# One unit ahead of the second chunk's scores, and group 1's output products one step sooner

## The chip, the cores and the metric

The kernel runs on one core of a Trainium2 chip. A core has five engines with in-order instruction streams of their own: TensorE (matmuls and weight loads, PE and PEld in the profile), VectorE (DVE), ScalarE (ACT), GpSimd (POOL) and SyncE (SP); they are tied together by semaphores, and 16 DMA engines move data. Matmuls write into PSUM, which has eight banks of 512 float32 per partition. The metric is the device time of one execution in microseconds, the median of several.

## The reference

Two parts, one behind the other. A linear attention with a decay per head, in blocks of 64 tokens:

```
for each block b of 64 tokens:                       # q, k, v: [4, 8, 768, 64]
    intra = (qb kb^T * Dmask) vb                     # within the block, decayed by lam^(i-j)
    inter = (qb * lam^(i+1)) kv_state                # with all blocks before
    out[block] = intra + inter
    kv_state = lam^64 * kv_state + (kb * lam^(63-i))^T vb
x = out, heads side by side                          # [3072, 512]
h = x @ w_in                                         # [3072, 2048]
g = h + sin(alpha * h)^2 / (alpha + 1e-9)
result = g @ w_out                                   # [3072, 512], float32
```

## The kernel before

The 768 tokens of a sequence are cut into six chunks of 128 (t = 0 to 5), each of two blocks of 64. The chunk t of all four sequences makes group t of 512 tokens for the second part. So that TensorE always has something to do, the second part of group g runs beside the attention of chunk g + 1 (`t = g + 1`). All instructions are issued in an order that the program writes out by hand; each engine takes its own instructions in that order.

**The second part.** A group has 16 steps, one for each 128 of the 2048 hidden columns. `hidden(g, i)` (line 538) issues four matmuls of 512 columns into a PSUM bank `hps` (line 542), then a sine (547) and a square (552) on ScalarE; `finish(g, i)` (line 557) adds the hidden value and writes `gall` on VectorE (561), and thereby frees the bank. In group 1, banks 0 to 2 go round from step 4 on, so that step 12 takes the bank of step 9, step 13 that of step 10 and step 14 that of step 11; step 15 takes bank 4. The product with w_out is cut into *units*: `project(g, m, part)` (line 567) is four matmuls (572) for the m-th 128 tokens and the part-th quarter of the hidden columns; with part 3 the result is copied out and stored. Units wait in the list `behind`, and `run(n)` (line 687) issues the next n of them, wherever the program wants TensorE filled.

**The attention of a chunk**, in the order of its steps:

- loads of k, q, v through GpSimd's queue; k and q turned (heads to partitions) either by TensorE with a copy on ScalarE (`turns_pair`, lines 338 to 344) or by a DMA transpose from SyncE's queue (273);
- `pair_ready`: decayed keys on GpSimd (257); `states` (423): key-value products on TensorE; `update`: new state on VectorE (399, 403), decayed and cast on GpSimd (388, 392);
- `scores` (443): TensorE writes F_ps; `masks` (450): VectorE multiplies by the decay table and writes STm;
- output products into O_ps: those with the state (457) and those with the scores (482 or 505). For chunk 1 they are split over `outputs_first` and `outputs`; from chunk 2 on `outputs_in_one` (line 487 on) issues all, 64 of each kind. One product with the state is held until a small ScalarE copy of part of the turned q (`seen`, lines 472 and 516), a *fence*, which itself waits for the products issued ahead of it;
- `leave` (524): VectorE multiplies O_ps and writes x, the input of the next group (*x copies*), four for a chunk: pair 0 of the sequences and pair 1, each for two blocks.

**Chunk 1 (the second chunk).** Its attention runs between group 0 and group 1, in a straight list of calls (lines 722 to 751) with `run(n)` between them. After the last q is turned (`turns_pair(1, "q", 2, 5, (A, A))`) come its ScalarE copies, one unit, `update`, `scores`, `masks`, `outputs_first`, two units, `outputs`, `leave`, two units.

**Group 1 (with chunk 2).** For each step i the loop at line 802 issues what `feed` has for it, `hidden(1, i)`, what `slots` has for it, the units of this step, and `finish(1, i)`. Scores and masks come at steps 8 and 9 into and out of banks 4 to 7, which the output products use again. `hidden` takes a call `ahead`, which it makes between its four matmuls and its sine: at one step (`here`) of group 1 this is `outputs_in_one(2)`. Units come at steps 1, 3, 4, 8, 10 and 13; the one at step 13 multiplies the columns of steps 8 to 11. Groups 2 to 4 make the same call between sine and square of step 11 (`between`).

Of the kernel before, what the change touches and what calls it, by code (L numbers as in the profile page):

```python
# [15 lines left out]
def kernel(  # L16
# [16 lines left out]
    NT = S // T  # L33
# [61 lines left out]
    def load(t, nm, b0, b1):  # L95
        dst, src = NAT[nm]
        to = dst[t][:, b0:b1, :, :].rearrange("p b h e -> p (b h) e")
        by_head = src[b0:b1, :, t * T:(t + 1) * T, :].rearrange("b h p e -> p (b h) e")
        n = H * (b1 - b0)
        if t > 1 and nm != "v" and b0 == 2:  # L100
            nc.gpsimd.dma_start(out=to[:, 0:n - 1, :], in_=by_head[:, 1:n, :])
            nc.gpsimd.dma_start(out=to[:, n - 1:n, :], in_=by_head[:, 0:1, :])
        else:
            nc.gpsimd.dma_start(out=to, in_=by_head)  # L104
# [141 lines left out]
    def new_xt(t):  # L246
        xt[t] = xtp.tile([P, NDC, GRP], BF16, name="xt")
# [179 lines left out]
    def update(t, blk, pr):  # L427
        if blk and t == NT - 1:
            return
        new_state(blk, pr, att["KV", t, pr, blk], "fused" if t == blk == 1 else "decayed")  # L430
        if t > 1 and (t, blk) != (NT - 1, 0):
            decay_state(blk, pr)
        cast_state(blk, pr, home(t + 1, 0) if blk else home(t, 1))
# [40 lines left out]
    def outputs(t, prs=BOTH):  # L474
        inter(t, prs[0], 0, 0, 0, False)
        for pr in prs:
            for h0 in range(0, 2 * H, 2):
                for blk in range(2):
                    for n in (h0, h0 + 1):
                        half, m = where(t, pr, n)  # L480
                        u, h = n // H, n % H
                        nc.tensor.matmul(out=att["O", t, pr, blk][halves(h % 2), u, h // 2, :],  # L482
                                         lhsT=vn[t][halves(blk), 2 * pr + u, h, :],
                                         rhs=STm[t, pr][halves(blk), half, m // HP, m % HP, :],
                                         start=False, stop=True, skip_group_check=True)

    def outputs_in_one(t):
        banks_of("O", t, BOTH, None, "O_ps")
        regions = [(pr, h0 + j, blk) for h0 in range(0, 2 * H, 2) for blk in range(2) for pr in BOTH for j in range(2)]

        def meets(straight):
            return [(pr, blk, n) + where(t, pr, n) for pr, n, blk in regions
                    if (where(t, pr, n)[0] == blk) == straight]

        begun = set()

        def with_state(of):
            for pr, blk, n, half, m in of:
                inter(t, pr, half, m, blk, (pr, half, blk) not in begun)
                begun.add((pr, half, blk))  # L500

        def with_scores(of):
            for pr, blk, n, half, m in of:
                u, h = n // H, n % H
                nc.tensor.matmul(out=att["O", t, pr, blk][halves(h % 2), u, h // 2, :],  # L505
                                 lhsT=vn[t][halves(blk), 2 * pr + u, h, :],
                                 rhs=STm[t, pr][halves(blk), half, m // HP, m % HP, :],
                                 start=False, stop=True, skip_group_check=True)

        crossed, straight = meets(False), meets(True)  # L510
        sent = [r for r in crossed if (r[0], r[3], r[4]) == (0, 0, 0)]
        kept = [r for r in straight if (r[0], r[3], r[4]) == (0, 0, 0)]
        assert len(sent) == len(kept) == 1 and sent[0][1] == 1
        with_state([r for r in crossed if r not in sent] + sent)
        seen = QT[t][LO, 0, 0, 0:T:D]
        nc.scalar.copy(out=seen, in_=seen)
        with_state([r for r in straight if r not in kept])
        with_scores(straight)
        with_state(kept)
        with_scores(crossed)  # L520
# [158 lines left out]
    def queue_units(g, order):  # L679
        for m, part in order:  # L680
            def unit(g=g, m=m, part=part):
                project(g, m, part)
                if part == 3:
                    store(g, m)
            behind.append(unit)

    def run(n):
        for _ in range(min(n, len(behind))):
            behind.pop(0)()
# [46 lines left out]
    run(1)  # L736
    turns_pair(1, "q", 2, 5, (A, A))
    load(2, "k", 0, 2)
    run(1)
    update(1, 1, 1)  # L740
    scores(1, (1,), (5, 0))
    masks(1, 1)
# [1 line left out]
    outputs_first(1, (1,), (4, 2))  # L744
    load(2, "q", 0, 2)
    load(2, "q", 2, 4)
    run(2)
    outputs(1, (1,))
    leave(1, 1)
    run(2)  # L750
# [3 lines left out]
    def slots(g):  # L754
        t = g + 1
        d = {i: [] for i in range(NFC)}
        if g == 1:
            at = dict(KV=5, F=9, O=12)
        else:
            at = dict(KV=4, F=8, O=12)  # L760
        d[at["KV"]] += [(states, t)]
        for n in range(4):
            d[at["KV"] + ((0, 0, 1, 2)[n] if g == 1 else n)] += [(update, t, n // 2, n % 2)]
        if g == 1:
            d[8] += [(run, 1), (scores, 2), (masks, 2, 0)]
        else:
            d[at["F"]] += [(scores, t), (masks, t, 0)]
        d[at["F"] + (g > 1)] += [(masks, t, 1)]
        d[at["O"]] += [(leave, t, 0)]
        d[at["O"] + (g > 1)] += [(leave, t, 1)]  # L770
        return d

    def feed(g):
        t = g + 1
        d = {i: [] for i in range(NFC)}
        if g == 1:
            d[2] += [(turn_by_dma, 2, 0, "k"), (pair_ready, 2, 1), (decay_state, 1, 0), (decay_state, 1, 1), (turn_by_dma, 2, 1, "k"), (turn_by_dma, 2, 0, "q")]
            d[7] += [(put_held,), (turns_pair, 2, "q", 2, AB[0], (A, A))]
        if t + 1 < NT:
            if g == 1:  # L780
                d[6] += [(new_chunk, 3)] + [(load, 3, nm, b, b + 2) for nm, b in (("v", 0), ("k", 0), ("v", 2))]
                d[7] += [(load, 3, nm, b, b + 2) for nm, b in (("k", 2), ("q", 0), ("q", 2))]
            else:
                a = 6 if g == 2 else 2
                d[a] += [(new_chunk, t + 1)] + [(load, t + 1, nm, b, b + 2) for nm, b in (("v", 0), ("k", 0), ("v", 2))]
                d[a + 2] += [(load, t + 1, nm, b, b + 2) for nm, b in (("k", 2), ("q", 0), ("q", 2))]
            d[12] += [(turn_by_dma, t + 1, 0, "k"), (turn_by_dma, t + 1, 1, "k")]
            d[13] += [(pair_ready, t + 1, 0)]
            d[14] += [(turn_by_dma, t + 1, 0, "q"), (turn_by_dma, t + 1, 1, "q")]
            d[15] += [(pair_ready, t + 1, 1)]  # L790
        return d

    for g in range(1, NT + 1):
        if g < NT:
            gall[g] = gbp.tile([P, NFC, GRP], BF16, name="gall")
        at = slots(g) if g + 1 < NT else {}
        fd = feed(g) if g + 1 < NT else {}
        if g + 1 < NT:
            new_xt(g + 1)
        own = {8: (0, 0), 10: (0, 1), 13: (0, 2)} if g == 1 else {}  # L800
        units = [1, 3, 4, 10, 13] if g == 1 else [i for i in range(NFC) if g > 2 or i not in (0, 1, 3)]
        for i in range(NFC):
            if g == NT and not behind:
                break
            if i in own:
                queue_units(g, [own[i]])
            for a in fd.get(i, []):
                a[0](*a[1:])
            here = g + 1 < NT and i == (12 if g == 1 else 11)

            def unit_and_outputs():
                run(1)
                outputs_in_one(g + 1)

            if g < NT:
                hidden(g, i, unit_and_outputs if here and g > 1 else None,
                       (lambda: outputs_in_one(2)) if here and g == 1 else None)
            for a in at.get(i, []):
                a[0](*a[1:])
            if not (here and g > 1):  # L820
                run(units.count(i))
            if g < NT:
                finish(g, i)
        if g < NT:
            queue_units(g, [(m, part) for m in range(B - 1 if g == NT - 1 else B) for part in range(4)][len(own):])
# [31 lines left out]
```

## Time and profile before

| | |
|---|---|
| median of 3 runs (lowest to highest) | 207.53 us (207.43 to 207.54) |
| profiled execution | 207.3 us |
| its span, first to last instruction | 205.5 us |
| TensorE busy, matmuls | 197.5 us (96%) |
| ScalarE busy | 142.9 us (70%) |
| VectorE busy | 131.5 us (64%) |
| GpSimd busy | 106.7 us (52%) |
| granted TensorE clock, mean | 1.000 |

The profile is of one execution. Times in it are microseconds from the span's start. In a list in order of time, a row can hold several instructions of the same kind behind each other (x4), and the brackets tell how long the engine was idle before the row and whose end it waited for. A matmul's end is modelled and overlaps the next one's start: matmuls of 512 columns that follow each other start 0.216 us apart (20 from 70.17 to the next row at 74.49), though one is shown 0.38 us long. Some matmul records are missing, so a row of four can read x3.

### The profile page before, as it was taken

The numbers are of one execution on the slowest core, as the hardware profiler recorded it, in microseconds if no ns is written. First come the engines' busy times: TensorE is split into PE (matmuls) and PEld (weight loads), VectorE is DVE, ScalarE is ACT, GpSimd is POOL, SyncE is SP. The second block draws the span as 40 slices with busy tenths as digits, with TensorE's granted clock in tenths as the row PEclk, the third lists the DMA queues.
The fourth block names the chain that finished last, engine by engine and source line by source line (L and its number), as shares of the span: only waits on it lengthen the run. The fifth ranks groups of instructions, "written<-read, shape, count | busy, mean of one in ns | idle before, by whom it ended". The sixth has DMA issues, their size and how long they took to land.

```text
span 205.5 us, 5388 instructions
## 1 busy us (share of the span) xinstructions
PE 197.5 (96%) x2239; PEld 98.4 (48%) x2265; DVE 131.5 (64%) x219; ACT 142.9 (70%) x241; POOL 106.7 (52%) x112
## 2 busy tenths in 40 slices
PE   7899999999998999999999999999999999999994
PEld 2664455554453545455445454444454444444443
DVE  7695989473889769968557968555858544444000
ACT  7688997224999699676776676776676787887121
POOL 8989959988979973999976940002000000000000
PEclk9999999999999999999999999999999999999999
DMA  8999999999979999699999989601101101110213
GB/s 132 160 179 206 205 160 177 187 178 156 165 263 98 135 153 181 43 169 162 120 137 146 212 99 154 155 3 51 54 0 54 51 0 54 53 51 0 104 51 105
DMA packets 96683, 24.49 MB, mean 119 GB/s; under 512 B 87938, under 2 KB 94226, under 8 KB 96658
## 3 DMA queue, kind: packets, MB, share of 16 engines
q0 software_dynamic: 74528, 13.37, 86.8%
q1 hardware_dynamic: 22128, 10.76, 24.9%
q8 instruction: 18, 0.29, 0.6%
q14 instruction: 7, 0.06, 0.1%
q10 hardware_dynamic: 2, 0.00, 0.0%
HBM read 27.27 MB, written 6.29 MB: 163 GB/s over the span
## 4 chain that ended last, share of the span: by engine, by line
PE 88%; DMA 3%; ACT 2%; DVE 2%; POOL 2%; issue 1%; POOLq 0%; ACTq 0%
PE hps L542 38%; PE ops L572 38%; DMA qn<-in_q_dram 3%; PE O_ps L457 2%; PE hps L597 2%; PE KV_ps L423 2%; POOL kn L104 1%; PE F_ps L443 1%; DVE STm L450 1%; PE O_ps L505 1%; DVE gall L561 1%; PE hps L139 1%; ACT QKT L344 1%; ACT s_sb L547 1%; PE O_ps L363 1%
## 5 line engine op out<-in xcount | busy, mean ns | idle before, releaser
L561 DVE SCALAR_TENSOR_TENSOR gall<-s,r_sb,hps 128x512 bf16<-128x512 bf16 x96 | 71.1, 745 | 44.7 <-ACT s L552 44.5
L542 PE MATMUL hps<-xt,w_in 128*128 128x512 bf16 x370 | 94.0, 379 | 1.7 <-DVE gall L561 0.8
L572 PE MATMUL ops<-w_out,gall 128*128 128x512 bf16 x356 | 90.8, 379 | 1.1 <-issue 0.5
L547 ACT ACTIVATE s_sb<-hps,alpha_sb 128x512 bf16<-128x512 f32 x96 | 65.3, 684 | 29.6 <-PE hps L542 28.4
L552 ACT ACTIVATE s<-s_sb 128x512 bf16<-128x512 bf16 x91 | 57.3, 630 | 2.8
L542 PEld LDWEIGHTS <-w_in 128*128 128x128 bf16 x384 | 36.6, 98 | 44.0 <-issue 1.6
L572 PEld LDWEIGHTS <-gall 128*128 128x128 bf16 x368 | 34.9, 98 | 41.2 <-issue 0.6
L257 POOL TENSOR_TENSOR kdec<-kn,R 128x1024 bf16<-128x1024 bf16 x12 | 22.8, 1915 | 3.8 <-DMA kn<-in_k_dram 2.3
L392 POOL CAST sb<-S 128x512 bf16<-128x512 f32 x20 | 12.3, 619 | 21.1 <-DVE S L399 21.1
L388 POOL TENSOR_TENSOR SD<-S,L 128x512 f32<-128x512 f32 x16 | 16.7, 1049 | 8.6 <-DVE S L399 8.5
L524 DVE TENSOR_TENSOR xt<-O_ps,Etab 128x512 bf16<-128x512 f32 x20 | 12.8, 684 | 5.4 <-PE O_ps L482 4.4
L104 POOL DMA_DIRECT2D vn<-in_v_dram x13 | 14.6, 1122 | 0.0
L579 DVE COPY o_sb<-ops 128x512 f32<-128x512 f32 x15 | 10.3, 689 | 4.2 <-PE ops L572 4.1
L450 DVE TENSOR_TENSOR STm<-F_ps,C 128x512 bf16<-128x512 f32 x20 | 12.8, 683 | 0.3 <-PE F_ps L443 0.3
L581 ACT COPY o_sb<-ops 128x512 f32<-128x512 f32 x8 | 4.6, 577 | 12.0 <-PE ops L572 12.0
L399 DVE TENSOR_TENSOR S<-SD,KV_ps 128x512 f32<-128x512 f32 x16 | 10.8, 683 | 0.1
L104 POOL DMA_DIRECT2D kn<-in_k_dram x9 | 9.9, 1097 | 0.3 <-issue 0.3
L344 ACT COPY QKT<-T_ps 128x512 bf16<-128x512 bf16 x8 | 4.3, 584 | 5.3 <-PE T_ps L341 5.3
L139 PE MATMUL hps<-fill 128*128 128x256 bf16 (+1 forms) x24 | 6.5, 390 | 1.5 <-DVE fill L132 1.5
L104 POOL DMA_DIRECT2D qn<-in_q_dram x6 | 7.1, 1177 | 0.0
L356 DVE TENSOR_TENSOR STm<-F_ps,C 128x512 bf16<-128x512 f32 x8 | 5.2, 686 | 1.6 <-PE F_ps L352 1.5
L457 PEld LDWEIGHTS <-sb 64*64 64x64 bf16 x320 | 4.2, 107 | 3.0 <-issue 3.0
(95 smaller groups left out, 116.5 us busy)
## 6 DMA issues: line engine op xcount, KB each, us to landing
out_dram<-o_sb SPq DMA_DIRECT2D x19, 256.0 KB, 2.6
vn<-in_v_dram POOLq DMA_DIRECT2D x10, 256.0 KB, 8.1
w_out<-in_moe_w_out_dram POOLq DMA_DIRECT2D x4, 512.0 KB, 10.7
w_in<-in_moe_w_in_dram POOLq DMA_DIRECT2D x3, 512.0 KB, 9.8
kn<-in_k_dram POOLq DMA_DIRECT2D x6, 256.0 KB, 8.2
qn<-in_q_dram POOLq DMA_DIRECT2D x6, 256.0 KB, 9.0
out_dram<-o_sb SPq DMA_DIRECT2D x8, 128.0 KB, 1.8
kn<-in_k_dram POOLq DMA_DIRECT2D x4, 240.0 KB, 6.5
```

Source lines behind the costliest of these rows:

```text
L104: nc.gpsimd.dma_start(out=to, in_=by_head)
L257: nc.gpsimd.tensor_tensor(out=kdec[t][:, b0:b1, :, :], in0=kn[t][:, b0:b1, :, :], in1=R[:, o:o + H].unsqueeze(1).unsqueeze(3).broadcast_to ...
L388: nc.gpsimd.tensor_tensor(out=pair(SD, pr), in0=pair(S_of[n], pr), op=ALU.mult, in1=L64[:, pr].unsqueeze(1).unsqueeze(3).broadcast_to([P, ...
L392: nc.gpsimd.tensor_copy(out=pair(dst, pr), in_=pair(S_of[n], pr))
L399: nc.vector.tensor_tensor(out=S, in0=pair(SD, pr), in1=ps, op=ALU.add)
L450: nc.vector.tensor_tensor(out=st[:, hd], in0=att["F", t, pr, hd], op=ALU.mult, in1=of_mask(C64, t, pr, hd).unsqueeze(1).broadcast_to([P, 2 ...
L524: nc.vector.tensor_tensor(out=xview(t)[:, 2 * pr:2 * pr + 2, blk, :, :], in0=att["O", t, pr, blk], in1=Eb, op=ALU.mult)
L542: nc.tensor.matmul(out=hps[:], lhsT=w[:, c, (f % 4) * P:(f % 4 + 1) * P], rhs=xt[g][:, c, :], start=(c == 0), stop=(c == NDC - 1))
L547: nc.scalar.activation(out=s_sb[:], in_=hps[:], func=ACTF.Sin, scale=alpha_sb[:, f:f + 1])
L552: nc.scalar.activation(out=s2[:], in_=s_sb[:], func=ACTF.Square)
L561: nc.vector.scalar_tensor_tensor(out=gall[g][:, f, :], in0=s2[:], scalar=r_sb[:, f:f + 1], in1=hps[:], op0=ALU.mult, op1=ALU.add)
L572: nc.tensor.matmul(out=ops[:], lhsT=gall[g][:, f, m * P:(m + 1) * P], rhs=w_out_sb[part][:, f % 4, :], start=(f == 0), stop=(f == NFC - 1))
```

## The change

Two edits, both of order alone; every engine executes the same instructions as before.

In chunk 1, one of the two units between `outputs_first` and `outputs` moves to the place between the last turned q and the scores: two units there, one here.

In group 1, `outputs_in_one(2)` is called at step 11 instead of step 12, between the four matmuls of the step and its sine. On TensorE the output products thus stand ahead of step 12's matmuls; on ScalarE the fence's copy stands ahead of the twelfth sine (step 11) instead of the thirteenth. The x copies, all four ahead of the finish of step 12 before, become two ahead of the finish of step 11 and two ahead of that of step 12. The orders of GpSimd and SyncE do not change.

```diff
@@ chunk 1 @@
     turns_pair(1, "q", 2, 5, (A, A))
     load(2, "k", 0, 2)
-    run(1)
+    run(2)
     update(1, 1, 1)
     scores(1, (1,), (5, 0))
     masks(1, 1)
...
     load(2, "q", 2, 4)
-    run(2)
+    run(1)
     outputs(1, (1,))
     leave(1, 1)
@@ slots(g) @@
         if g == 1:
-            at = dict(KV=5, F=9, O=12)
+            at = dict(KV=5, F=9, O=11)
...
         d[at["O"]] += [(leave, t, 0)]
-        d[at["O"] + (g > 1)] += [(leave, t, 1)]
+        d[at["O"] + 1] += [(leave, t, 1)]
@@ loop over the steps @@
-            here = g + 1 < NT and i == (12 if g == 1 else 11)
+            here = g + 1 < NT and i == 11
```

## The prediction

> **What bounds the kernel now.** I read the page first: the shares of busy time and the slices of the span.
>
> ```profile
> span 205.5 us, 5388 instructions
> PE 197.5 (96%) x2239; PEld 98.4 (48%) x2265; DVE 131.5 (64%) x219; ACT 142.9 (70%) x241; POOL 106.7 (52%) x112
> PEclk9999999999999999999999999999999999999999
> PE 88%; DMA 3%; ACT 2%; DVE 2%; POOL 2%; issue 1%; POOLq 0%; ACTq 0%
> ```
>
> TensorE is busy for 96% of the span at full granted clock, and the chain of waits, the last line, runs through it for 88%. The change adds and removes no matmul, so it can only fill or open holes in TensorE's row. I therefore went to the order in time of each engine around the two edited places. Columns: start, duration, engine, line; in brackets the idle time before and its releaser. First the second chunk, between the last turned q and its output products:
>
> ```profile
> 42.41 1.04 PE L572 MATMUL ops<-w_out,gall 128*128 128x512 bf16 x4
> 43.64 0.45 PE L443 MATMUL F_ps<-QKT 64*64 64x64 bf16 x32 [0.20 <-ACT QKT L344]
> 44.74 1.67 PE L572 MATMUL ops<-w_out,gall 128*128 128x512 bf16 x7 [0.16 <-issue]
> 46.35 0.21 PE L457 MATMUL O_ps<-QKT,sb 64*64 64x64 bf16 x1
> ...
> 43.37 0.10 PEld L443 LDWEIGHTS <-QKT 64*64 64x64 bf16 x1 [0.42 <-issue]
> ...
> 42.52 1.07 ACT L344 COPY QKT<-T_ps 128x512 bf16<-128x512 bf16 x2 [3.00 <-PE T_ps L341]
> ...
> 44.14 1.29 DVE L450 TENSOR_TENSOR STm<-F_ps,C 128x512 bf16<-128x512 f32 x2 [0.30 <-PE F_ps L443]
> 46.88 1.29 DVE L524 TENSOR_TENSOR xt<-O_ps,Etab 128x512 bf16<-128x512 f32 x2 [1.45 <-PE O_ps L482]
> ```
>
> The scores (F_ps) start at 43.64, when ScalarE's two copies of the turned q end (42.52 + 1.07 = 43.59). Their first weights were loaded at 43.37, so one unit of four matmuls covers the copies all but 0.27 us.
>
> Then group 1, steps 11 to 14 (hps rows):
>
> ```profile
> 61.02 0.74 PE L443 MATMUL F_ps<-QKT 64*64 64x64 bf16 x64
> 64.34 1.02 PE L542 MATMUL hps<-xt,w_in 128*128 128x512 bf16 x4
> 66.20 1.02 PE L542 MATMUL hps<-xt,w_in 128*128 128x512 bf16 x4 [0.83 <-DVE gall L561]
> 67.15 0.71 PE L457 MATMUL O_ps<-QKT,sb 64*64 64x64 bf16 x63
> 68.00 0.21 PE L457 MATMUL O_ps<-QKT,sb 64*64 64x64 bf16 x1
> 68.44 1.04 PE L542 MATMUL hps<-xt,w_in 128*128 128x512 bf16 x3
> 69.31 1.03 PE L572 MATMUL ops<-w_out,gall 128*128 128x512 bf16 x4
> 70.17 4.48 PE L542 MATMUL hps<-xt,w_in 128*128 128x512 bf16 x20
> ...
> 69.09 0.75 PEld L572 LDWEIGHTS <-gall 128*128 128x128 bf16 x4
> ...
> 64.21 1.28 DVE L450 TENSOR_TENSOR STm<-F_ps,C 128x512 bf16<-128x512 f32 x2
> 65.41 2.13 DVE L561 SCALAR_TENSOR_TENSOR gall<-s,r_sb,hps 128x512 bf16<-128x512 bf16 x3
> 68.57 2.48 DVE L524 TENSOR_TENSOR xt<-O_ps,Etab 128x512 bf16<-128x512 f32 x4 [1.04 <-PE O_ps L505]
> 70.97 1.40 DVE L561 SCALAR_TENSOR_TENSOR gall<-s,r_sb,hps 128x512 bf16<-128x512 bf16 x2
> ...
> 64.74 0.63 ACT L552 ACTIVATE s<-s_sb 128x512 bf16<-128x512 bf16 x1
> 65.40 0.69 ACT L547 ACTIVATE s_sb<-hps,alpha_sb 128x512 bf16<-128x512 f32 x1
> 66.12 0.63 ACT L552 ACTIVATE s<-s_sb 128x512 bf16<-128x512 bf16 x1
> 67.67 0.20 ACT L516 COPY QKT<-QKT 64x2 bf16<-64x2 bf16 x1 [0.91 <-PE O_ps L457]
> 67.77 0.68 ACT L547 ACTIVATE s_sb<-hps,alpha_sb 128x512 bf16<-128x512 f32 x1
> ```
>
> Step 11 issues from 64.34; step 12 could follow at 65.20 but starts at 66.20, 1.00 us later, because its bank (2) is freed by VectorE's finish of step 9, the first of three at 65.41, which stood behind the masks. TensorE has nothing else queued there; the output products come after step 12.
>
> **Part 1, the unit moved ahead of the scores.** Unit, scores, output products and the later unit keep their counts and their transitions; only the copies' cover changes. A unit takes 0.86 (69.31 to 70.17). After the change the scores could start 0.86 past 43.37, at 44.23, long after the copies end at 43.59: the wait of 0.27 goes. Behind the scores one unit instead of two stands ahead of the output products, so these would start at 46.35 − 0.27 = 46.08. They need the masks, which now run 0.50 behind the scores' start (43.64 to 44.14) for 1.29: from 44.73 to 46.02. So 0.06 is left; that is late next, and beyond it the wait returns one for one. The small ScalarE copy after the first output products (the second chunk's fence) still has a unit of 0.86 behind it. Bounds: 0.37 (from 43.27, the issue end of the unit, to 43.64) and 0.1 (masks 0.2 later than worked out). I take 0.27, by the weight row.
>
> The x copies of 46.88, and with them all of group 1, start earlier by that much. Nothing there hangs on a transfer: the rows below carry that.
>
> A page rule beside this: the Trainium skill, "TensorE: Matmul & The Clock Gate", section "Back-to-back issue gap", gives about 131 ns for each matmul of 512 columns in a sustained stream. By it a unit would take 0.52, the copies would stick out by 0.6 and filling would gain 0.52, for a sum of some −1.3 instead of −1.0; the trace's 0.86 for four (216 ns each) contradicts it, and I go by the trace.
>
> **Part 2, the output products ahead of step 12.** On before's clock: after step 11 they could begin at 64.34 + 0.95 (as 66.20 to 67.15) = 65.29. They write banks 4 to 7, which the masks read; the last mask ends at 64.21 + 1.28 = 65.49, and TensorE follows 0.05 later, as at 66.20 (65.41 + 0.74 = 66.15). So some 0.25 of the hole stays and they start at 65.54. They last 1.29 (67.15 to 68.44), to 66.83. Step 12 starts there, 0.63 later than now but without a wait (bank 2 free at 66.15), step 13 at 66.83 + 0.86 = 67.69 instead of 68.44: **0.75 gained**.
>
> What the fence costs: its copy ran 0.52 after the products began (67.15 to 67.67), so it now runs at 66.06; ScalarE's eleventh square ends at 65.37, so nothing delays it. The one product it holds stood 0.85 behind the first (68.00), that is 66.39, against a copy done at 66.26: no wait. Queued behind it on ScalarE is the twelfth sine, 0.10 behind the copy (67.67, 67.77): 66.16 instead of 65.40, its square done 1.35 later (65.40 to 66.75), at 67.51. A sine starts 1.06 behind its first matmul (64.34, 65.40) and takes 1.32 with its square (0.69 + 0.63): step 12's at 67.89, step 13's at 69.21 instead of 68.75, step 14's at 70.53 where its matmuls (from 69.42) would allow 70.48. ScalarE is even by step 14.
>
> What the split copies cost on VectorE: finish of step 10 runs in its old place. The first pair of x copies started 0.13 behind step 13 (68.44, 68.57), now 0.13 behind step 12, at 66.96, 0.60 each (68.57 to 70.97 for four); then finish of step 11 from 68.16 to 68.90. Two wait for that: the fourth matmul of the unit at step 13, whose weights are those columns (the unit starts at 68.55, its fourth weight load at 68.55 − 0.22 + 0.65 = 68.98), and step 14's bank at 69.42. So 0.08 is left at the unit: tight, late next here, and free by 0.5 at step 14. The second pair ends at about 70.0; group 2's first step, which needs them all, issues at 71.1. Step 15's bank (4) is left by the first pair at 67.6.
>
> Bounds of part 2: 1.00 (the whole hole, were the masks no obstacle) and 0.45 (the unit at step 13 stalls by 0.3).
>
> **What follows.** With 1.02 gained, TensorE asks earlier for what GpSimd and the transfers bring:
>
> ```profile
> 57.68 1.04 POOL L388 TENSOR_TENSOR SD<-S,L 128x512 f32<-128x512 f32 x1 [1.36 <-DVE S L399]
> 72.15 3.79 POOL L257 TENSOR_TENSOR kdec<-kn,R 128x1024 bf16<-128x1024 bf16 x2
> 80.24 1.04 POOL L388 TENSOR_TENSOR SD<-S,L 128x512 f32<-128x512 f32 x1 [4.30 <-DVE S L399]
> ...
> 77.17 0.74 PE L423 MATMUL KV_ps<-vn,kdec 64*64 64x64 bf16 x64
> 115.49 0.74 PE L443 MATMUL F_ps<-QKT 64*64 64x64 bf16 x64
> ...
> L273 SPq DMA_TRANSPOSE QKT<-qn x2: 1232/1654/2075, 76.3 to 77.6; - x2
> ...
> DMA to landing us min/median/max: 3.9/4.0/4.1
> L273 SPq DMA_TRANSPOSE QKT<-qn x1: 2464/2464/2464, 105.4 to 105.4; - x1
> ...
> DMA to landing us min/median/max: 9.1/9.1/9.1
> ...
> sum 117.00, PE 116.26 PEld 55.40 DVE 72.34 ACT 82.05 POOL 37.66; mean PE 29.07 PEld 13.85 DVE 18.09 ACT 20.51 POOL 9.42
> ```
>
> The rows with L273 are DMA issues (durations, first and last start) and the line under each tells from issue to landing; the last row sums the busy time of each engine from 78 to 195 us.
>
> GpSimd's eighteen instructions from 57.68 to 72.15 + 3.79 = 75.94 (loads of chunk 3, then decayed keys; first and last row shown) follow each other without a gap, started by VectorE's state, so it moves with part 1 to 75.67; the chunk-3 states, now at 77.17 − 1.02 = 76.15, need the second half of it: free by half a us. GpSimd's next stretch, 80.24 on, with all loads of chunk 4, waits for VectorE and so moves by the whole gain, and the queue of DMA issues and SyncE with it. The last turned q of chunk 4 lands at 105.4 + 9.1 = 114.5, 1.0 ahead of its scores at 115.49, and moves along. Behind that nothing waits, so the gain reaches the end.
>
> **Sum.** −0.27 − 0.75 = −1.02. The profiled execution took 207.3 (span 205.5 and 1.8 around it): 206.28. It lies 0.23 under the median of the runs, 207.53, so the prediction there is **206.5 us**. Bounds: all upper ends, −1.37, give 206.16; all lower ones, −0.55, 206.98.
>
> **Rivals.** Two tenths of a per cent is 0.41 us, about what a measurement can tell from no change.
>
> Only the second part pays: the masks, now last before the output products at 46.08, come 0.27 late. For it speaks the margin of 0.06; against it that VectorE is free from its last state update to them. −0.75: 206.8.
>
> The first-in-first-out rival: the fence holds the twelfth sine and the first x copies hold its finish, and the unit at step 13 and step 14 stall for it. The thirteenth sine, in the place that the twelfth takes, started at 67.77 though its matmuls ended at 66.20 + 1.02 = 67.22, so the holding is real; from my 0.08 on, each delay of the finish of step 11 costs as much. If that takes the 0.75, part 1 remains: 207.3, no measurable change. The Trainium skill, "Perfetto Trace Analysis", section "Tensor Engine Instruction", says that ScalarE, VectorE and GpSimd are strictly first in, first out while TensorE may pull weight loads ahead; the row of the held sine agrees, and so does the load at 69.09, 0.22 ahead of its matmul.
>
> Slower: chunk 4's last turned q. The same two issues of chunk 3 landed in 3.9 and 4.1, so landings swing by 5 us with what they overlap. If moving the stores and loads against each other delays it by more than 1.0 plus what TensorE gained, scores of chunk 4 set the end; at 1.5 us past their present place of 115.49 the time is 209.0. It decides from a landing at 115.9 (slower by 0.41); 114.5 and moving the other way speak against it.
>
> No effect: a wait that I have not seen elsewhere in groups 2 to 5 takes the gain, 207.5. Against it, TensorE is busy for 116.26 of the 117.00 from 78 to 195, so no wait there ends last now.
>
> **Chances.** Both parts 0.62; only part 2 0.10 (with the first, faster: 0.72, and 0.02 for half of part 2). Fence and copies give it back 0.09 and no effect 0.04: same 0.13. Slower 0.13. The range runs from 206.0 (all upper ends and 0.15 for the scatter of medians) to 207.4, which takes in the rival of the fence; the likeliest case alone is 206.2 to 206.9.
>
> **What would show it.** Scores of the second chunk with no idle time before them and eight unit matmuls ahead; output products there at about 46.1. In group 1 the output products next behind step 11, at about 65.3 (65.54 less 0.27), the copy at 65.8, the twelfth sine just behind it, x copies in two pairs with one finish between; no idle above 0.2 at the unit of step 13. From chunk 3's states on, all of TensorE's rows 1.0 earlier. A stall of TensorE at step 13's unit or at the scores of chunk 4, or the masks of the second chunk ending behind 46.1, makes it wrong.

## The result

| | before | after |
|---|---|---|
| median of 6 runs (lowest to highest), us | 207.53 (207.43 to 207.90) | 206.64 (206.52 to 206.84) |
| ratio, 95% interval | | 0.9955 (0.9942 to 0.9968) |
| profiled execution, us | 207.3 | 206.68 |
| its span, us | 205.5 | 204.9 |

The change makes the kernel 0.89 us (0.45%) faster; 206.5 was forecast. Beside the experiments the changed kernel was run again: 206.63, ratio 0.9953 (0.9935 to 0.9971).

**The profile after.** The page reads 98% for TensorE instead of 96. That is no measure of the gain: 26 of 2265 matmul records are missing in the profile before (x2239), and none here.

```profile
span 204.9 us, 5414 instructions
PE 200.1 (98%) x2265; PEld 98.5 (48%) x2265; DVE 132.0 (64%) x219; ACT 142.7 (70%) x241; POOL 106.5 (52%) x112
```

The instructions in order of time, of the changed kernel, in the second chunk (TensorE, then VectorE):

```profile
42.81 1.90 PE L572 MATMUL ops<-w_out,gall 128*128 128x512 bf16 x8
44.64 0.45 PE L443 MATMUL F_ps<-QKT 64*64 64x64 bf16 x32
45.51 1.04 PE L572 MATMUL ops<-w_out,gall 128*128 128x512 bf16 x4
46.48 0.21 PE L457 MATMUL O_ps<-QKT,sb 64*64 64x64 bf16 x1
...
45.14 1.29 DVE L450 TENSOR_TENSOR STm<-F_ps,C 128x512 bf16<-128x512 f32 x2 [0.91 <-PE F_ps L443]
```

The wait for ScalarE's copies ahead of the scores is gone; from the first unit behind the last turned q to the held output product it is 46.48 − 42.81 = 3.67 us, against 46.35 − 42.41 = 3.94 before. The masks end at 45.14 + 1.29 = 46.43, 0.05 ahead of their use.

And in group 1, steps 11 to 14 (TensorE, its weight loads, ScalarE, VectorE):

```profile
64.50 1.02 PE L542 MATMUL hps<-xt,w_in 128*128 128x512 bf16 x4
65.45 0.92 PE L457 MATMUL O_ps<-QKT,sb 64*64 64x64 bf16 x63
66.52 0.21 PE L457 MATMUL O_ps<-QKT,sb 64*64 64x64 bf16 x1
66.95 1.90 PE L542 MATMUL hps<-xt,w_in 128*128 128x512 bf16 x8
68.69 1.03 PE L572 MATMUL ops<-w_out,gall 128*128 128x512 bf16 x4
69.56 4.48 PE L542 MATMUL hps<-xt,w_in 128*128 128x512 bf16 x20
...
68.48 0.74 PEld L572 LDWEIGHTS <-gall 128*128 128x128 bf16 x4
...
66.18 0.20 ACT L516 COPY QKT<-QKT 64x2 bf16<-64x2 bf16 x1 [0.66 <-PE O_ps L457]
66.28 0.68 ACT L547 ACTIVATE s_sb<-hps,alpha_sb 128x512 bf16<-128x512 f32 x1
...
64.36 1.28 DVE L450 TENSOR_TENSOR STm<-F_ps,C 128x512 bf16<-128x512 f32 x2
67.09 1.29 DVE L524 TENSOR_TENSOR xt<-O_ps,Etab 128x512 bf16<-128x512 f32 x2
68.29 0.74 DVE L561 SCALAR_TENSOR_TENSOR gall<-s,r_sb,hps 128x512 bf16<-128x512 bf16 x1
```

The output products stand directly behind step 11. Their first row lasts 0.92 instead of 0.71: that 0.21 is what is left of the hole, the wait for the last mask (64.36 + 1.28 = 65.64). Narrower windows of the same list split the row there (65.4 to 65.5, then 65.68 to 66.1): two products run, and the others follow from 65.70 on.

```profile
65.45 0.22 PE L457 MATMUL O_ps<-QKT,sb 64*64 64x64 bf16 x2
...
65.70 0.58 PE L457 MATMUL O_ps<-QKT,sb 64*64 64x64 bf16 x49
```

Steps 12 and 13 follow without a gap, and so does the unit. From step 11 to the unit of step 13 it is 68.69 − 64.50 = 4.19 us, against 4.97 before.

**Where to measure from.** The two profiles do not start alike: the first unit behind the last turned q comes at 42.81 after and at 42.41 before, though up to there both execute the same instructions in the same order. I call that moment U. The last product (L597) is the other end:

```profile
199.01 3.66 PE L597 MATMUL hps<-w_out,gall 128*128 128x384 bf16 x32
```

```profile
198.39 3.66 PE L597 MATMUL hps<-w_out,gall 128*128 128x384 bf16 x32
```

From U to there it is 156.60 us before (first row) and 155.58 after (second): 1.02 less, of which 0.40 is hidden in this pair of profiles by the later start. What comes behind the last product, with what lies around the span, is 207.3 − 199.01 = 8.29 before and 206.68 − 198.39 = 8.29 after. So a profiled time is U + the stretch + 8.29 (8.28 to 8.32 in all nine profiles), and only the stretch tells of the change. The table gives both for every kernel that was run; "step 13" is the unit there (L572 at 68.69 above).

| kernel | U | U to held product, chunk 1 | U to step 13 | U to last product | median | ratio (95%) |
|---|---|---|---|---|---|---|
| before | 42.41 | 3.94 | 26.90 | 156.60 | 207.53 | |
| changed | 42.81 | 3.67 | 25.88 | 155.58 | 206.64 | 0.9955 (0.9942 to 0.9968) |
| changed, again | 42.85 | 3.68 | 25.86 | 155.57 | 206.63 | 0.9953 (0.9935 to 0.9971) |
| unit alone | 43.44 | 3.67 | 26.69 | 156.40 | 207.38 | 0.9996 (0.9984 to 1.0007) |
| products alone | 42.75 | 3.94 | 26.13 | 155.83 | 206.65 | 0.9958 (0.9945 to 0.9970) |
| four x copies first | 42.78 | 3.67 | 25.85 | 156.52 | 207.51 | 0.9996 (0.9983 to 1.0010) |
| three units first | 42.67 | 3.99 | 26.70 | 156.40 | 207.38 | 0.9993 (0.9984 to 1.0002) |
| x copies late | 42.93 | 3.68 | 25.85 | 155.57 | 206.57 | 0.9951 (0.9933 to 0.9969) |
| fence behind the sine | 42.37 | 3.67 | 25.86 | 155.57 | 206.49 | 0.9946 (0.9928 to 0.9964) |

The runs of the kernel before that go with the ratios had medians of 207.57 (rows four to seven) and 207.64 (again, and the last two). The stretch of the kernel before is known from one profile, but both of its waits recur where one part of the change is left out: 3.94 with the products alone, and 4.96 from step 11 to the unit of step 13 with the unit alone (65.17 to 70.13, below).

The forecast gave its places on the clock of the profile before. To compare, 0.40 comes off the times after: the second chunk's output products are at 46.08 (46.1 forecast) and the end of its masks at 46.03, within the 46.1 that was set as the limit; in group 1 the products that need the last mask are at 65.30 (65.3) and the fence's copy at 65.78 (65.8).

### The profile page after: what moved, and what is told of

It is laid out like the page before. It is cut to its first block, busy times and chain, and to the rows that moved or that the text cites. A ratio compares the mean times of both kernels' runs of the same rounds, so it can differ in the third digit from the quotient of the medians.

```text
span 204.9 us, 5414 instructions
## 1 busy us (share of the span) xinstructions
PE 200.1 (98%) x2265; PEld 98.5 (48%) x2265; DVE 132.0 (64%) x219; ACT 142.7 (70%) x241; POOL 106.5 (52%) x112
## 4 chain that ended last, share of the span: by engine, by line
PE 96%; DVE 2%; ACT 0%; issue 0%; ACTq 0%
PE hps L542 41%; PE ops L572 40%; PE O_ps L457 2%; PE hps L139 2%; PE KV_ps L423 2%; PE hps L597 2%; PE F_ps L443 2%; PE T_ps L305 1%; PE O_ps L505 1%; PE T_ps L320 1%; DVE xt L370 1%; PE F_ps L352 1%; PE T_ps L338 1%; DVE STm L356 1%; PE KV_ps L380 0%
## 5 line engine op out<-in xcount | busy, mean ns | idle before, releaser
L542 PE MATMUL hps<-xt,w_in 128*128 128x512 bf16 x384 | 95.5, 379 | 0.3 <-DVE xt L370 0.3
L572 PE MATMUL ops<-w_out,gall 128*128 128x512 bf16 x368 | 92.1, 379 | 0.0
L572 PEld LDWEIGHTS <-gall 128*128 128x128 bf16 x368 | 34.8, 98 | 41.7 <-issue 0.9
```

Of the source, the lines that this page charges most:

```text
L542: nc.tensor.matmul(out=hps[:], lhsT=w[:, c, (f % 4) * P:(f % 4 + 1) * P], rhs=xt[g][:, c, :], start=(c == 0), stop=(c == NDC - 1))
L572: nc.tensor.matmul(out=ops[:], lhsT=gall[g][:, f, m * P:(m + 1) * P], rhs=w_out_sb[part][:, f % 4, :], start=(f == 0), stop=(f == NFC - 1))
```

## The experiments

The first two cuts of code below are against the kernel before, the other four against the changed kernel; `...` marks lines left out.

**The two parts one by one.** The unit alone:

```diff
     load(2, "k", 0, 2)
-    run(1)
+    run(2)
     update(1, 1, 1)
...
-    run(2)
+    run(1)
     outputs(1, (1,))
```

> The unit moved ahead of the second chunk's scores, and nothing else. My theory: the scores no longer wait, the output products there start 2.00 us behind the last turned q's first unit... worked on the rows: from the first unit behind the last turned q to the held output product 3.67 us instead of 3.94 (42.41 to 46.35), so 0.27 us faster than before, 207.26; in group 1 the hole of 0.8 to 0.9 us ahead of step 12 stays. Rival, the masks come late and take it back: 3.94 us, and 207.53.

The order of TensorE in time:

```profile
43.44 1.90 PE L572 MATMUL ops<-w_out,gall 128*128 128x512 bf16 x8
47.11 0.21 PE L457 MATMUL O_ps<-QKT,sb 64*64 64x64 bf16 x1
...
65.17 1.02 PE L542 MATMUL hps<-xt,w_in 128*128 128x512 bf16 x4
67.02 1.02 PE L542 MATMUL hps<-xt,w_in 128*128 128x512 bf16 x4 [0.83 <-DVE gall L561]
...
70.13 1.03 PE L572 MATMUL ops<-w_out,gall 128*128 128x512 bf16 x4
```

In the second chunk the gain is what was expected, 3.94 to 3.67, and the hole ahead of step 12 stands untouched at 0.83. To the last product 0.20 arrives instead of 0.27; the rest goes between the second chunk and the scores of group 1, where this execution, whose U is 0.5 to 1.1 later than the others', spent 0.07 more on the states of chunk 2 (57.11 to 57.84, against 56.53 to 57.19 in the second profile of the changed kernel); why is not shown. The medians (207.57 to 207.38, interval of the ratio through 1) cannot confirm so small a gain.

The products alone:

```diff
-            at = dict(KV=5, F=9, O=12)
+            at = dict(KV=5, F=9, O=11)
-        d[at["O"] + (g > 1)] += [(leave, t, 1)]
+        d[at["O"] + 1] += [(leave, t, 1)]
-            here = g + 1 < NT and i == (12 if g == 1 else 11)
+            here = g + 1 < NT and i == 11
```

> Group 1's output products at step 11 with the fence ahead of the twelfth sine and the x copies in two steps, the unit left where it was. My theory: from step 11's first matmul to the unit of step 13 4.22 us instead of 4.97 (64.34 to 69.31), 0.75 us faster than before, 206.78; the second chunk keeps its wait of 0.27. Rival, the fence and the copies give it back: 4.97 us and 207.53. Were the two parts not independent, the two gains would not add to the 0.9 to 1.0 of both.

```profile
42.75 1.04 PE L572 MATMUL ops<-w_out,gall 128*128 128x512 bf16 x4
43.98 0.44 PE L443 MATMUL F_ps<-QKT 64*64 64x64 bf16 x32 [0.20 <-ACT QKT L344]
...
64.68 1.02 PE L542 MATMUL hps<-xt,w_in 128*128 128x512 bf16 x4
68.88 1.03 PE L572 MATMUL ops<-w_out,gall 128*128 128x512 bf16 x4
```

From step 11 to the unit 4.20 us instead of 4.97, and the scores of the second chunk wait as before. The stretch to the last product is 0.77 shorter than before's, the ratio 0.9958 clear of 1. The two parts add: 0.20 and 0.77 against 1.02 for both. By the medians nearly all comes from the second part (206.65 beside 206.64); the 0.25 by which the stretches differ is of the size by which U moves between executions.

**What stands ahead of the finish of step 11.** With all four x copies first:

```diff
         d[at["O"]] += [(leave, t, 0)]
-        d[at["O"] + 1] += [(leave, t, 1)]
+        d[at["O"] + (g > 1)] += [(leave, t, 1)]
```

> The changed kernel, but with all four x copies ahead of the finish of step 11. This doubles what stands ahead of that finish on VectorE. My theory: the finish of step 11 comes 1.2 us later, its margin at the unit of step 13 is 0.1, so TensorE stalls for about 1.1 us ahead of that unit's fourth matmul and all but the gain of the unit is lost: 207.7. Rival, the finish has slack and the split into two steps does nothing: 206.64 as the changed kernel.

TensorE, then VectorE:

```profile
66.90 1.90 PE L542 MATMUL hps<-xt,w_in 128*128 128x512 bf16 x8
68.63 0.81 PE L572 MATMUL ops<-w_out,gall 128*128 128x512 bf16 x3
70.23 0.39 PE L572 MATMUL ops<-w_out,gall 128*128 128x512 bf16 x1 [0.78 <-DVE gall L561]
...
67.03 2.48 DVE L524 TENSOR_TENSOR xt<-O_ps,Etab 128x512 bf16<-128x512 f32 x4
69.43 2.06 DVE L561 SCALAR_TENSOR_TENSOR gall<-s,r_sb,hps 128x512 bf16<-128x512 bf16 x3
```

The unit starts when it did, its first three matmuls run, and the fourth waits until the finish of step 11 ends at 69.43 + 0.74 = 70.17. The stretch grows by 0.94 over the changed kernel's (1.1 was expected), and the time is 207.51: the whole gain of the second part is gone. So what stands ahead of this finish on VectorE is a condition of that gain. It does not have to be this split, though. With all four behind the finish of step 11:

```diff
-        d[at["O"]] += [(leave, t, 0)]
+        d[at["O"] + (g == 1)] += [(leave, t, 0)]
         d[at["O"] + 1] += [(leave, t, 1)]
```

> The changed kernel, but with all four x copies behind the finish of step 11, at step 12. My theory: the finish of step 11 is then set by its square alone and comes 0.6 us earlier, the copies end at about 70.8 on the clock of the changed kernel's first profile, 0.4 us ahead of group 2's first step at 71.3, so nothing waits: 206.64, and the split into two steps matters only against having all four first. Rival, group 2's first step waits for the copies: up to 0.5 us slower.

```profile
67.75 0.75 DVE L561 SCALAR_TENSOR_TENSOR gall<-s,r_sb,hps 128x512 bf16<-128x512 bf16 x1 [0.70 <-ACT s L552]
68.41 2.48 DVE L524 TENSOR_TENSOR xt<-O_ps,Etab 128x512 bf16<-128x512 f32 x4
```

The finish now waits only for its square and comes 0.66 earlier (24.82 behind U instead of 25.48), the copies end at 70.89, and the stretch is 155.57, that of the changed kernel. Here the finish must not stand behind four copies; behind two or none it comes in time.

**The place of the fence**, between the twelfth sine and its square instead of ahead of the sine:

```diff
-                hidden(g, i, unit_and_outputs if here and g > 1 else None,
-                       (lambda: outputs_in_one(2)) if here and g == 1 else None)
+                hidden(g, i, unit_and_outputs if here and g > 1 else (lambda: outputs_in_one(2)) if here else None)
```

> The changed kernel, but with the fence behind the twelfth sine instead of ahead of it. My theory: the sine then starts at 65.55 instead of 66.28 and ends at 66.2, just when the fence could run; the held product at 66.52 does not wait for it, and the finish of step 11 stays behind the x copies: 206.64, no change beyond 0.1 us either way. Rival, the place of the fence matters: the sine delays the fence and TensorE waits for the held product, 0.2 us or more slower; or the earlier square makes it faster by as much.

ScalarE, then TensorE:

```profile
65.09 0.69 ACT L547 ACTIVATE s_sb<-hps,alpha_sb 128x512 bf16<-128x512 f32 x1
65.72 0.20 ACT L516 COPY QKT<-QKT 64x2 bf16<-64x2 bf16 x1
65.82 0.62 ACT L552 ACTIVATE s<-s_sb 128x512 bf16<-128x512 bf16 x1
...
66.06 0.21 PE L457 MATMUL O_ps<-QKT,sb 64*64 64x64 bf16 x1
66.49 1.90 PE L542 MATMUL hps<-xt,w_in 128*128 128x512 bf16 x8
```

The sine fits into the time in which the copy had to wait anyway, and the copy ends (65.92) ahead of the held product (66.06). The stretch is 155.57 once more: the place is free. Its lowest median of all, 206.49, goes with ratios that overlap; its profile has the earliest U (42.37) and no shorter stretch, so nothing here makes it the faster kernel.

**How far units can be moved ahead of the scores.** All three:

```diff
     load(2, "k", 0, 2)
-    run(2)
+    run(3)
     update(1, 1, 1)
...
-    run(1)
     outputs(1, (1,))
```

> The changed kernel, but with the third unit too moved ahead of the second chunk's scores, so that none stands between its output products. My theory: the masks start with the end of the scores, 0.86 us later, and nothing covers them: the held output product starts 0.85 us later than in the changed kernel, 207.5. Rival, the masks are covered otherwise: 206.64.

TensorE, then VectorE:

```profile
42.67 2.76 PE L572 MATMUL ops<-w_out,gall 128*128 128x512 bf16 x12
45.36 0.45 PE L443 MATMUL F_ps<-QKT 64*64 64x64 bf16 x32
46.66 0.19 PE L457 MATMUL O_ps<-QKT,sb 64*64 64x64 bf16 x1 [0.35 <-ACT QKT L472]
47.20 0.45 PE L482 MATMUL O_ps<-STm,vn 64*64 64x64 bf16 x32 [0.36 <-DVE STm L450]
...
45.86 1.29 DVE L450 TENSOR_TENSOR STm<-F_ps,C 128x512 bf16<-128x512 f32 x2 [1.77 <-PE F_ps L443]
```

Without a unit between its output products TensorE waits twice: for the fence's copy and then for the masks, which end at 45.86 + 1.29 = 47.15. The expectation named the held product; that one comes 0.32 later than in the changed kernel (3.99 behind U instead of 3.67), and it is the products with the scores behind it that come 0.86 later (4.53 instead of 3.67). The stretch is 0.82 longer than the changed kernel's (0.85 expected), 207.38. So nearly all of the unit that stayed is needed: its 0.86 covers the masks with 0.05 to spare.

## Why the prediction was right

- **Part 1, 0.27.** Right: 3.94 to 3.67 in the second chunk. The margin at the masks, forecast 0.06, is 0.05, and one unit more shows the wait behind it. In the whole, 0.20 of it is seen alone and 0.25 on top of the second part, too little for the medians to show.
- **Part 2, 0.75.** Right: 4.97 to 4.19 from step 11 to the unit of step 13, 0.77 to the end when alone. The rest of the hole for the masks was forecast as 0.25 and is 0.21.
- **The fence.** Forecast 0.52 behind the first output product and not waited for; it came at 66.18, 0.73 behind, because the mask's wait falls inside the first products (behind two of them) and not ahead of all, and it was not waited for. The twelfth sine is indeed just behind it (66.28), 0.7 later than it could have run, and ScalarE is even by step 14.
- **The tight place.** Forecast: 0.08 left at the fourth weight load of the unit at step 13. The finish of step 11 ends at 68.29 + 0.74 = 69.03; the four loads run from 68.48 on for 0.74, the fourth for the last 0.10 of it, from 69.12: 0.09 left. The first-in-first-out rival was therefore a real one with its condition not met; four copies meet it.
- **What follows.** The rows below, of the changed kernel, are chunk 3's states with GpSimd's decayed keys, and the scores of chunk 4 with the last turned q.

```profile
76.56 0.74 PE L423 MATMUL KV_ps<-vn,kdec 64*64 64x64 bf16 x64
114.87 0.74 PE L443 MATMUL F_ps<-QKT 64*64 64x64 bf16 x64
...
72.28 3.79 POOL L257 TENSOR_TENSOR kdec<-kn,R 128x1024 bf16<-128x1024 bf16 x2
...
L273 SPq DMA_TRANSPOSE QKT<-qn x1: 2983/2983/2983, 103.6 to 103.6; - x1
...
DMA to landing us min/median/max: 9.8/9.8/9.8
```

The keys end at 76.07, half a us ahead of the states, as forecast. The last turned q lands at 103.6 + 9.8 = 113.4, 1.5 ahead of the scores: the rival on the slower side did not come near.

- **The sum.** 1.02 forecast, 1.02 measured from U to the last product. That they agree to the hundredth is in part chance: of the 0.27 only 0.24 is left at step 11 (from U to there 21.93 before, 21.69 after), and part 2 then gives 0.78 and not 0.75. The medians give 0.89 and, in the other set, 1.01. The forecast's 206.5 missed the median by 0.14. It carried over the 0.23 between before's profile and its median as if it were fixed, while in the profiles such tenths lie ahead of U, where the change does nothing, and 42.41 is an early U. For the executions of which only the time is known, this is argued and not shown.

## What to carry to other kernels

A hole in the bounding engine can be filled by whatever is next in its own order and does not depend on what the hole waits for; the gain is the hole less the new work's own wait, and both can be read to a tenth of a us from the rows in order of time. Then look at who stands in the queues behind the moved work: the same move was worth 0.77 us with the x copies in two pairs and nothing with all four ahead of one finish. When a small gain is to be seen, measure between two moments that enclose the edit, not over the whole execution. The other way to close the hole in group 1, the finish of step 9 ahead of the last two masks on VectorE, was not tried.

## What was not expected

The start of the kernel scatters more than its whole remainder. Up to U all kernels here execute the same instructions, and U lies between 42.37 and 43.44 in nine profiles, while the stretch from U to the last product agrees within 0.01 us between the two profiles of the changed kernel and the two variants that left its path alone (155.57, 155.57, 155.57, 155.58). What TensorE waits for on the way to U changes from execution to execution. The rows are of the unit alone (TensorE, then VectorE), of the x copies late, and of the changed kernel's second profile:

```profile
7.19 0.61 PE L295 MATMUL T_ps<-iden,qn 128*128 128x128 bf16 x4 [0.89 <-DVE qn L615]
6.44 0.69 DVE L615 TENSOR_TENSOR qn<-raw_q,Rq 128x512 bf16<-128x512 f32 x1 [1.10 <-DMA raw_q<-in_q_dram]
...
16.19 1.90 PE L542 MATMUL hps<-xt,w_in 128*128 128x512 bf16 x8 [0.77 <-DMA w_in<-in_moe_w_in_dram]
...
27.76 1.04 PE L572 MATMUL ops<-w_out,gall 128*128 128x512 bf16 x4 [0.90 <-DMA w_out<-in_moe_w_out_dram]
```

The late load is q in the first, w_in in the second and w_out in the third. So an early start need not last: the third began group 0 at 15.37, against 15.80 in the first profile of the changed kernel, and reached U at 42.85, against 42.81. Why a load comes late in one execution and not in another is not shown.
